# Two chunks side by side in a linear-attention stage, and ranks by two products

## The chip, the cores and the metric

The kernel runs on one core of a Trainium2 chip. The metric is the time of one execution on the device in microseconds; the median of three runs is compared. Names of engines: TensorE (PE; its weight loads are PEld), VectorE (DVE), ScalarE (ACT), GpSimd (POOL) and SyncE (SP), which issues most of the DMAs.

## The reference

The first stage is a retention layer (linear attention with a decay per head) for 4 batches, 8 heads, 768 steps and a head size of 64. Its output, seen as 3072 tokens of 512 features, goes through a mixture of 8 experts: each token goes to its best expert alone.

```python
for t in range(S):
    state = gamma[None, :, None, None] * state + np.einsum('bhd,bhe->bhde', k[:, :, t], v[:, :, t])
    y[:, :, t] = scale * np.einsum('bhd,bhde->bhe', q[:, :, t], state)
...
logits = x @ w_gate + modality_bias[modality_id]
e_idx = np.argmax(logits, axis=1)
...
for e in range(E):
    mask = e_idx == e
    h = np.maximum(x[mask] @ w1[e], 0.0)
    out[mask] = gate_w[mask, None] * (h @ w2[e])
```

## The kernel before, in words

**Retention.** The sequence is cut into chunks of 128 steps: 6 a batch, 24 in all (`NN`). For chunk n the kernel needs five kinds of TensorE products. `scores(n)` (L164) multiplies k and q of all heads, two heads at a time in the two halves of the rows (64*128), into two PSUM banks; VectorE applies the causal mask, which gives the tile `a` (L176). `heads_out(n)` (L182) makes the output y: first the state times q (L189, array of 64*64, four at once; left out in the first chunk of a batch), then v times `a` (L195, 128*64), both into the same two banks; VectorE multiplies them by the decay and writes `yT` (L202). `state(n)` (L222) adds k times v of chunk n to a bank that lives for a batch (L227, 128*64; left out in the last chunk of a batch), and ScalarE copies it to `s` (L232). `tokens_out(n)` (L205) multiplies yT by a matrix that holds the identity and the gate weights (L213, 128*128), in two halves u that have a bank each; ScalarE copies them to `xs`, and VectorE adds up the logits `lg` (L218). GpSimd makes `vd`, v with its decay (L159), ScalarE makes `dq`, the decay for the output (L152).

**The order.** All engines but GpSimd issue exactly in the order of the Python code (`manual_schedule`), GpSimd in the order of its pinned instructions. `retention(n)` (L869) does, on TensorE: state of n, scores of n+1, x of n-1, y of n. Loads are issued on SP nine chunks ahead (`LEAD`); k and q, and k and v, go to rooms that the weights and hidden tiles of the experts use later. Between the steps stand hooks: `at(n, where, ...)` places a function at a point of chunk n ("top", "st", "sc", "pr", "tk", "end").

**Ranking.** Every three chunks make a group. `route_a(g, 0)` and `route_a(g, 1)` (L299) are a serial chain of small VectorE steps: logits plus bias (L303), maximum, one-hot rows `oh`, and the running counts `cnt`. `route_b(g)` (L333) makes each token's place by five products: `upper` times `oh`, a base for each expert (`ebase`), the counts, and two sums over earlier chunks of the group. `route_c` and `route_a(g, 2)` (L349, L327) read the result on VectorE (`rkt`, `pos`, `den`, and three reciprocals). `scatter` (L358) writes each chunk's rows to a list of rows by expert in DRAM (`xsl`). After the group of chunk 11, `early_a` and `early_b` (L440, L448) pick two experts that have a full slot of 512 rows already: one product `pte` and 15 small VectorE steps from `full` to `bid`; `taken_a`, `taken_b` (L474, L479) note it with the tile `tk` and the products `ptk`.

**Experts.** Six jobs of 512 rows follow: two early ones (e0, e1) and four more (f0 to f3), each 192 products of 128x512. `flip` (L668) transposes a job's rows, `cut` (L657) splits weights into a high and a low part, `first` (L680) and `second` (L699) are the two layers. The flips and cuts of e0 are hooks in the last chunks of the retention, with the low parts on GpSimd (L663). `last_tokens` (L898) and the final lists (`final_a` to `final_d`) run between the first products of e0. Small remainders of experts (`rest_*`, L739 to L806) and rows that fill gaps (`gaps_*`) run in between.

Of the kernel before, what the change touches and what calls it, by code (L numbers as in the profile page):

```python
# [40 lines left out]
LEAD = 9  # L41
XSB = 6
# [3 lines left out]
C_ID, C_MASK, C_DEC, C_IOTA, C_FAC, C_GRP, C_LANE, C_END = 0, 128, 256, 304, 312, 336, 337, 356  # L46
# [3 lines left out]
def kernel(  # L50
# [44 lines left out]
    run_base = cst[:, C_LANE + 3 + NE : C_LANE + 3 + 2 * NE]  # L95
# [4 lines left out]
    ebase = cp.tile([P, GRP, NE], BF16, name="ebase")  # L100
# [3 lines left out]
    cnt = [cp.tile([P, NE], BF16, name=f"cnt{i}") for i in range(NGRP + 1)]  # L104
# [6 lines left out]
    kqs, kts, vts, vds, lg, mid, xss = ({} for _ in range(7))  # L111

    kqr = ld.tile([P, 4, 2, DM], F32, tag="kq", name="kqr", bufs=1)


    def load_kq(n, split=False):
        i = n % 12
        if i < 4:
            t = kqr[:, i]
        else:  # L120
            t = me.tile([P, QW], F32R, tag=f"{('hi2', 'lo2')[i // 8]}{i % 4}", name=f"kq_{n}")
            t = t.bitcast(F32).rearrange("p (i d) -> p i d", i=2)
        kqs[n] = t
        if split:
            nc.sync.dma_start(t[:, 0], qkv[n][:, 0])
            nc.scalar.dma_start(t[:, 1], qkv[n][:, 1])
        else:
            nc.sync.dma_start(t, qkv[n][:, 0:2])
# [16 lines left out]
    def decay_q(n):  # L145

        c = n % NCH
        if c == 0:
            return dcq
        t = wk.tile([P, NG, P], F32, tag="dq", name=f"dq_{n}", bufs=1)  # L150
        for g in range(NG):
            nc.scalar.activation(t[:, g], dcq[:, g], AF.Copy, scale=fac[:, c, g : g + 1])  # L152
        return t

    def decay_v(n):
        vv = vts[n].rearrange("p (h e) -> p h e", h=H)
        vds[n] = wk.tile([P, H, D], F32, tag="vd", name=f"vd_{n}", bufs=2)
# [6 lines left out]
    def scores(n):  # L164
        kt, qt = (kqs[n][:, i].rearrange("p (g t) -> p g t", g=NG) for i in range(2))
        a = wk.tile([P, 2, NG, P], F32, tag="a", name=f"a_{n}")
# [13 lines left out]
        return a, qt  # L180

    def heads_out(n, a, vd, qv, s, dq):  # L182
        py = [bank(f"y{j}_{n}")[:, : 2 * P].rearrange("p (c t) -> p c t", c=2) for j in range(2)]
        if s is not None:
            for g in range(NG):
                for j in range(2):
                    r = slice(j * D, (j + 1) * D)
                    h = slice(g % 2 * D, (g % 2 + 1) * D)
                    nc.tensor.matmul(  # L189
# [936 lines left out]
```

## Time and profile before

| what | value |
|---|---|
| median of three runs | 408.42 us (407.78 to 408.92) |
| profiled execution | 407.8 us |
| its span, first to last instruction | 405.9 us |
| VectorE busy | 192.8 us |
| ScalarE busy | 155.0 us |
| GpSimd busy | 100.3 us |

An execution's time is about 1.9 us longer than its span: that is what lies around the instructions. Rows of the timeline give start, duration, engine, line, operation, out<-in, and the count of merged instructions; rows of the chain give start, duration, and what it stood on; rows of groups give a count, busy time, the mean of one in ns, and the idle time before it with what ended it. The ends of products on TensorE are modelled, so two that follow each other overlap in the rows; their starts are what to go by.

### The profile page before, as it was taken

To read this page: it belongs to the slowest core of one execution; us is meant where nothing else is said; L and a number is where in the kernel's file an instruction comes from. 1 tells how busy PE (TensorE), PEld (TensorE's weight loads), DVE (VectorE), ACT (ScalarE), POOL (GpSimd) and SP (SyncE) were. 2 spreads that over 40 slices of the span, in tenths; PEclk is the share of its full clock that TensorE was granted. 3 is DMA by queue.
4 is the path that set the end of the run, shared out by engine and by line. 5 is a ranking of instruction groups with operands and counts; after the bars stand their busy time and mean duration, and the time that the engine had idled before them with its cause. 6 is when DMAs were issued, how large, how long until landed. Compare 5 with 4: busy or idle time off the path is not lost.

```text
span 405.9 us, 8274 instructions
## 1 busy us (share of the span) xinstructions
PE 391.2 (96%) x3099; PEld 324.4 (80%) x3099; DVE 192.8 (48%) x489; ACT 155.0 (38%) x309; POOL 100.3 (25%) x120
## 2 busy tenths in 40 slices
PE   4999999999998999999999999999999999999993
PEld 3888888888886888888887888778888888888882
DVE  1687688879747932346214362143622463234200
ACT  1444544458543423335233252332523352243210
POOL 1326543578552471000110001100011000100011
PEclk9999999999999999999999999999999999999999
DMA  7999999984345484266971669616343453310011
GB/s 274 386 379 414 410 384 368 406 261 177 122 146 200 178 288 153 104 213 195 359 252 53 222 188 375 242 53 214 105 144 115 136 182 131 130 54 2 0 52 49
DMA packets 26795, 82.33 MB, mean 203 GB/s; under 512 B 4733, under 2 KB 4861, under 8 KB 26497
## 3 DMA queue, kind: packets, MB, share of 16 engines
q1 hardware_dynamic: 21328, 66.11, 45.9%
q0 software_dynamic: 5136, 15.21, 9.7%
q8 instruction: 26, 0.43, 0.4%
q10 hardware_dynamic: 288, 0.44, 0.3%
q14 instruction: 17, 0.14, 0.1%
HBM read 65.43 MB, written 23.41 MB: 219 GB/s over the span
## 4 chain that ended last, share of the span: by engine, by line
PE 58%; issue 32%; POOL 4%; DVE 2%; DMA 1%; POOLq 1%; ACT 0%; ACTq 0%; DVEq 0%
PE h_e L686 11%; PE o_e L704 11%; PE x L213 6%; PE sc L171 6%; PE h_f L686 6%; PE y L195 6%; PE o_f L704 4%; POOL out_dram L712 3%; PE y L189 3%; PE st L227 3%; DMA cst<-in_consts_dram 1%; PE xp_e L671 1%; PE xp_f L671 1%; POOL lo_e L663 1%; POOL vd L159 1%
## 5 line engine op out<-in xcount | busy, mean ns | idle before, releaser
L704 PE MATMUL o_f<-hi_f,hT_f 128*128 128x512 f32 x256 | 79.4, 391 | 0.0
L665 DVE TENSOR_TENSOR lo_f<-raw_f,hi_f 128x1024 fp32r<-128x1024 f32 x32 | 39.2, 1225 | 49.6 <-ACT hi_f L660 49.6
L704 PEld LDWEIGHTS o_f<-hi_f,hT_f 128*128 128x128 f32 x256 | 47.6, 188 | 9.6
L694 DVE SCALAR_TENSOR_TENSOR hT_f<-h_f,hT_f 128x512 fp32r<-128x512 f32 x32 | 22.1, 692 | 68.0 <-ACT hT_f L693 68.0
L686 PE MATMUL h_f<-xTh_f,hi_f 128*128 128x512 f32 x128 | 51.0, 399 | 0.0
L686 PE MATMUL h_f<-xTl_f,hi_f 128*128 128x512 f32 x128 | 50.2, 392 | 0.0
L686 PE MATMUL h_f<-xTh_f,lo_f 128*128 128x512 f32 x128 | 50.2, 392 | 0.0
L704 PE MATMUL o_f<-lo_f,hT_f 128*128 128x512 f32 x128 | 49.9, 390 | 0.0
L712 POOL DMA_INDIRECT out_dram<-o_f,tok_f x16 | 15.7, 979 | 133.1 <-ACT o_f L711 118.6
L693 ACT ACTIVATE hT_f<-h_f 128x512 fp32r<-128x512 f32 x32 | 19.1, 598 | 56.6 <-PE h_f L686 55.2
L176 DVE TENSOR_TENSOR a<-sc,cst 128x512 f32<-128x512 f32 x48 | 30.8, 684 | 19.2 <-PE sc L171 19.1
L704 PE MATMUL o_e<-hi_e,hT_e 128*128 128x512 f32 x128 | 39.8, 392 | 0.0
L159 POOL TENSOR_TENSOR vd<-kv,cst 128x512 f32<-128x512 f32 x24 | 25.1, 1045 | 38.4 <-PE y L195 23.7
L711 ACT ACTIVATE o_f<-o_f,gate_f 128x512 f32<-128x512 f32 x16 | 11.0, 689 | 59.9 <-issue 34.3
L660 ACT CAST hi_f<-raw_f 128x1024 fp32r<-128x1024 f32 x32 | 33.4, 1044 | 0.0
L366 POOL DMA_INDIRECT xsl<-xs,pos x24 | 24.4, 1017 | 27.5 <-DVE xs L330 14.4
L686 PEld LDWEIGHTS h_f<-xTh_f,hi_f 128*128 128x128 f32 x128 | 24.0, 188 | 6.4 <-issue 1.2
L213 PE MATMUL x<-wgt,yT 128*128 128x136 f32 x192 | 28.3, 290 | 0.5 <-DVE yT L202 0.5
L686 PEld LDWEIGHTS h_f<-xTl_f,hi_f 128*128 128x128 f32 x128 | 24.0, 188 | 5.5
L686 PEld LDWEIGHTS h_f<-xTh_f,lo_f 128*128 128x128 f32 x128 | 24.1, 188 | 5.1
L704 PEld LDWEIGHTS o_f<-lo_f,hT_f 128*128 128x128 f32 x128 | 24.0, 188 | 5.1
L704 PEld LDWEIGHTS o_e<-hi_e,hT_e 128*128 128x128 f32 x128 | 23.7, 188 | 4.7
(182 smaller groups left out, 623.4 us busy)
## 6 DMA issues: line engine op xcount, KB each, us to landing
raw_f<-in_w_dram SPq DMA_DIRECT2D x32, 512.0 KB, 3.4
kv<-in_qkv_dram SPq DMA_DIRECT2D x19, 512.0 KB, 11.0
kq<-in_qkv_dram SPq DMA_DIRECT2D x16, 512.0 KB, 10.6
raw_e<-in_w_dram SPq DMA_DIRECT2D x16, 512.0 KB, 4.3
xg_f<-xsl SPq DMA_DIRECT2D x16, 272.0 KB, 4.1
kqr<-in_w_dram SPq DMA_DIRECT2D x8, 512.0 KB, 4.6
rw<-in_w_dram SPq DMA_DIRECT2D x8, 512.0 KB, 6.4
kqr<-in_qkv_dram SPq DMA_DIRECT2D x7, 512.0 KB, 11.4
```

Source lines behind the costliest of these rows:

```text
L159: nc.gpsimd.tensor_tensor(vds[n], vv, dec[:, n % NCH].unsqueeze(2).to_broadcast([P, H, D]), op=ALU.mult)
L171: nc.tensor.matmul(pe[j][:, g * P : (g + 1) * P], kt[r, g], qt[r, g], start=True, stop=True, skip_group_check=True,)
L176: nc.vector.tensor_tensor(a[:, j], pe[j].rearrange("p (h t) -> p h t", t=P), mask.unsqueeze(1).to_broadcast([P, NG, P]), op=ALU.mult,)
L195: nc.tensor.matmul(py[j][g % 2 * D : (g % 2 + 1) * D, g // 2], vd[:, 2 * g + j], a[:, j, g], start=(s is None and g < 2), stop=(g >= 2), s ...
L213: nc.tensor.matmul(px[:, g], yT[:, 2 * u + g], wgt[:, 2 * u + g], start=(g == 0), stop=(g == 1), skip_group_check=True,)
L366: ins = nc.gpsimd.indirect_dma_start(out=xsl[:, :], out_offset=bass.IndirectOffsetOnAxis(ap=mid[gr][:, i : i + 1], axis=0), in_=xs.rearran ...
L660: nc.scalar.copy(hi, t)
L665: nc.vector.tensor_tensor(lo, t, hi.bitcast(F32), op=ALU.subtract)
L686: nc.tensor.matmul(s.ph, s.w[1][f // 2][wi][:, o : o + P], s.xT[kc][a], start=(kc == 0 and k == 0), stop=(kc == KC - 1 and k == 2),)
L694: nc.vector.scalar_tensor_tensor(lo, s.ph, 0.0, hi.bitcast(F32), op0=ALU.max, op1=ALU.subtract)
L704: nc.tensor.matmul(s.po, s.hT[f][a][:, hh * P : (hh + 1) * P], s.w[2][f // 2][wi][:, (f % 2) * DM : (f % 2 + 1) * DM], start=(f == 0 and k ...
L712: ins = nc.gpsimd.indirect_dma_start(out=out[:, :], out_offset=bass.IndirectOffsetOnAxis(ap=s.tok[:, hh : hh + 1], axis=0), in_=o[:, :], i ...
```

## The change

Chunks are taken two at a time. `two_chunks(n)` makes on TensorE the scores of n+2 and n+3, x of n-2 and n-1, the state products of y of n and n+1, and then `a` of n, state of n+2, `a` of n+1, state of n+3. `first_chunks()` starts this off. `a` has four rooms of one tile (`abuf`), `vd` four, `s` three, `dq` two, `xs` eight. Loads go twelve chunks ahead, into rooms of the weights (`hi`, `lo`), of xT and of hT; the tiles `kq` and `kv` of their own are gone, and the rests' weights go to `abuf`, `vd`, `yT` and `dq`. The count tiles hold the base of each expert from the start and the running sum before each chunk of the group (`cums`), so `route_b` needs two products; the constants of the lists are changed to suit. A group that is complete at an odd chunk is ranked one chunk later. The flips of e0 move from chunks 19 and 20 to 20 and 22. In `last_tokens` three empty steps are added and `final_a` moves behind `route_c`. The last output tile is scaled half on VectorE and half on ScalarE.

```diff
-LEAD = 9
-XSB = 6
+LEAD = 12
+XSB = 8
...
     def load_kq(n, split=False):
-        i = n % 12
-        if i < 4:
-            t = kqr[:, i]
-        else:
-            t = me.tile([P, QW], F32R, tag=f"{('hi2', 'lo2')[i // 8]}{i % 4}", name=f"kq_{n}")
-            t = t.bitcast(F32).rearrange("p (i d) -> p i d", i=2)
+        tag = f"{('hi', 'lo')[n // 4 % 2]}{1 if n < 8 else 2}{n % 4}"
+        t = me.tile([P, QW], F32R, tag=tag, name=f"kq_{n}")
+        t = t.bitcast(F32).rearrange("p (i d) -> p i d", i=2)
...
     def load_kv(n, split=False):
-        i = n % 10
-        if i < 8:
-            t = me.tile([P, 2, SLOT], F32R, tag=f"hT{i}", name=f"kv_{n}").bitcast(F32)
-        else:
-            t = ld.tile([P, 2, DM], F32, tag="kv", name=f"kv_{n}", bufs=2)
+        tag = f"xT{n - 8}" if n // 4 == 2 else f"hT{(n if n < 8 else n - 12) % 8}"
+        t = me.tile([P, 2, SLOT], F32R, tag=tag, name=f"kv_{n}").bitcast(F32)
...
-            new = sm.tile([P, NE], F32, tag="new", name=f"new_{gr}")
-            nc.vector.tensor_reduce(new, oh.rearrange("p c e -> p e c"), axis=AX.X, op=ALU.add)
-            nc.vector.tensor_tensor(cnt[gr + 1], cnt[gr], new, op=ALU.add)
+            cum = cums[gr]
+            for i in range(GRP):
+                nxt = cum[:, i + 1] if i + 1 < GRP else cnt[gr + 1]
+                nc.vector.tensor_tensor(nxt, cum[:, i], oh[:, i], op=ALU.add)
...
         nc.tensor.matmul(pr, upper, oh, start=True, stop=False, skip_group_check=True)
-        nc.tensor.matmul(
-            pr, ones[0:1, :], ebase[0:1], start=False, stop=False, skip_group_check=True
-        )
-        for i in range(-1, GRP - 1):
-            src = cnt[gr] if i < 0 else oh[:, i]
-            to = GRP - 1 - i
-            nc.tensor.matmul(
-                pr[:, i + 1 :], ones, src.unsqueeze(1).to_broadcast([P, to, NE]),
-                start=False, stop=(i == GRP - 2), skip_group_check=True,
-            )
+        nc.tensor.matmul(pr, ones, cums[gr], start=False, stop=True, skip_group_check=True)
...
         if part == 3:
-            nc.scalar.activation(o, s.po, AF.Copy, scale=s.gate[:, hh : hh + 1])
+            gate = s.gate[:, hh : hh + 1]
+            if s is jobs[-1] and hh == HH - 1:
+                h = DM // 2
+                nc.vector.tensor_scalar(o[:, h:], s.po[:, h:], gate, None, op0=ALU.mult)
+                nc.scalar.activation(o[:, :h], s.po[:, :h], AF.Copy, scale=gate)
+            else:
+                nc.scalar.activation(o, s.po, AF.Copy, scale=gate)
...
     for g in range(NGRP - 1):
         t = (g + 1) * GRP
+        t += t % 2
...
-        at(t + 7 + kc // 2, ("pr", "tk")[kc % 2], flip, e, kc)
+        at(t + 8 + kc // 2 * 2, ("pr", "tk")[kc % 2], flip, e, kc)
...
+    def two_chunks(n):
+        loads(n + LEAD - 2)
+        run(n, "top")
+        ahead = n + 2 < NN
+        if ahead:
+            decay_v(n + 2)
+        decay_q(n)
+        if ahead:
+            scores(n + 2)
+        run(n, "st")
+        loads(n + LEAD - 1)
+        if ahead:
+            scores(n + 3)
+            decay_v(n + 3)
+        run(n, "sc")
+        run(n, "pr")
+        tokens_out(n - 2)
+        run(n, "tk")
+        tokens_out(n - 1)
+        decay_q(n + 1)
+        run(n, "end")
+        run(n + 1, "top")
+        if n % NCH:
+            heads_s(n)
+        heads_s(n + 1)
+        run(n + 1, "st")
+        heads_a(n)
+        if ahead:
+            state(n + 2)
+        run(n + 1, "sc")
+        heads_a(n + 1)
+        run(n + 1, "pr")
+        if ahead:
+            state(n + 3)
+        run(n + 1, "tk")
+        run(n + 1, "end")
```

`heads_s` and `heads_a` are the two halves of `heads_out`, the first with the state, the second with `a` and the step to yT.

**TensorE in the middle of the retention.** Before, around chunks 8 and 9 (st state, sc scores, x tokens, y outputs, by chunk number):

```order
L227 MATMUL st_585<-vd_655,kv_139 64x64 x8
L171 MATMUL sc_9_759<-kq_156 128x128
...
L213 MATMUL x_0_772<-wgt,yT_714 128x136 x2
L213 MATMUL x_1_776<-wgt,yT_714 128x136 x2
L189 MATMUL y_8_781<-kq_137,s_665 64x128
...
L195 MATMUL y_8_781<-a_672,vd_655 64x128 x4
L195 MATMUL y_8_782<-a_672,vd_655 64x128 x4
L227 MATMUL st_585<-vd_737,kv_158 64x64 x8
L171 MATMUL sc_10_832<-kq_201 128x128
```

Now, in the pair of chunks 8 and 9:

```order
L166 MATMUL sc_10_762<-kq_148 128x128
...
L166 MATMUL sc_11_782<-kq_152 128x128
...
L219 MATMUL x_0_798<-wgt,yT_704 128x136 x2
L219 MATMUL x_1_802<-wgt,yT_704 128x136 x2
L219 MATMUL x_0_808<-wgt,yT_725 128x136 x2
L219 MATMUL x_1_812<-wgt,yT_725 128x136 x2
L190 MATMUL y_8_830<-kq_140,s_581 64x128
...
L190 MATMUL y_9_840<-kq_144,s_715 64x128
...
L202 MATMUL y_8_830<-abuf,vd_600 64x128 x4
L238 MATMUL st_551<-vd_755,kv_150 64x64 x8
L202 MATMUL y_9_840<-abuf,vd_634 64x128 x4
```

Blocks of one kind now stand next to each other for two chunks, and the state of chunk 10 stands between the two outputs.

**VectorE at the early list.** Before, behind the group of chunk 11 (yT of chunk 13, the list from `full` to `bid`, the ranking's second half from `rkt`, the note `tk`, then the masks of chunk 15):

```order
L202 TENSOR_TENSOR yT_1174<-y_13_1157,dq_1127 128x256
L451 TENSOR_TENSOR full_1185<-pte_1183,full_at 1x48
...
L352 TENSOR_TENSOR rkt_1211<-rk_1177,oh_1106 128x24
...
L476 TENSOR_SCALAR tk<-bid 1x48
L176 TENSOR_TENSOR a_1288<-sc_15_1289,cst 128x512
L176 TENSOR_TENSOR a_1288<-sc_15_1290,cst 128x512
```

Now:

```order
L209 TENSOR_TENSOR yT_1173<-y_13_1129,dq_1104 128x256
L452 TENSOR_TENSOR full_1191<-pte_1189,full_at 1x48
...
L353 TENSOR_TENSOR rkt_1217<-rk_1186,oh_1123 128x24
...
L171 TENSOR_TENSOR abuf<-sc_16_1234,cst 128x512
L171 TENSOR_TENSOR abuf<-sc_16_1235,cst 128x512
L477 TENSOR_SCALAR tk<-bid 1x48
L171 TENSOR_TENSOR abuf<-sc_17_1292,cst 128x512
L171 TENSOR_TENSOR abuf<-sc_17_1293,cst 128x512
```

The list and the second half stood ahead of one chunk's masks; now they stand ahead of the four masks of chunks 16 and 17, with `tk` in their midst. On TensorE the next pair's x of chunk 13, whose second half takes the bank that the first scores of chunk 16 leave, and then the products of `tk`, come after these scores:

```order
L166 MATMUL sc_17_1292<-kq_618 128x128
...
L219 MATMUL x_0_1312<-wgt,yT_1152 128x136 x2
L219 MATMUL x_1_1316<-wgt,yT_1152 128x136 x2
L219 MATMUL x_0_1322<-wgt,yT_1173 128x136 x2
L219 MATMUL x_1_1326<-wgt,yT_1173 128x136 x2
L483 LDWEIGHTS ones
L483 MATMUL ptk<-tk,ones 48x48
...
L190 MATMUL y_14_1351<-kq_429,s_1029 64x128
```

Before, these small products stood behind a chunk's outputs; now they stand between x and the outputs of the pair.

More of the change, by code (lines that the diff above doesn't have):

```diff
@@ L103 @@
     cnd = cp.tile([NCAND, 2 * NCAND + 3], F32, name="cnd")
-    cnt = [cp.tile([P, NE], BF16, name=f"cnt{i}") for i in range(NGRP + 1)]
+    cums = [cp.tile([P, GRP, NE], BF16, name=f"cum{i}") for i in range(NGRP + 1)]
+    cnt = [t[:, 0] for t in cums]
     def pin(ins):
@@ L179, in scores, with y_banks, heads_s, heads_a @@
             )
[L180 to L189, printed above, removed]
-                        py[j][h, g // 2], s[r, g], qv[r, g], start=(g < 2), stop=False,
-                        skip_group_check=True,
-                    )
+    def y_banks(n):
+        pys[n] = [
+            bank(f"y{j}_{n}")[:, : 2 * P].rearrange("p (c t) -> p c t", c=2) for j in range(2)
+        ]
+    def heads_s(n):
+        y_banks(n)
+        py, s = pys[n], ss.pop(n - 1)
+        qv = kqs[n][:, 1].rearrange("p (g t) -> p g t", g=NG)
+        for g in range(NG):
+            for j in range(2):
+                r = slice(j * D, (j + 1) * D)
+                h = slice(g % 2 * D, (g % 2 + 1) * D)
+                nc.tensor.matmul(
+                    py[j][h, g // 2], s[r, g], qv[r, g], start=(g < 2), stop=False,
+                    skip_group_check=True,
+                )
+    def heads_a(n):
+        first = n % NCH == 0
+        if first:
+            y_banks(n)
+        py, vd, a, dq = pys.pop(n), vds.pop(n), az.pop(n), dqs.pop(n)
         for j in range(2):
@@ L220, in tokens_out, with state @@
         )
-    def state(n, st, vd):
+    def state(n):
+        c = n % NCH
+        if c == NCH - 1:
+            return
+        if c == 0:
+            ss["st"] = bank(f"st_{n}")[:, : NG * D].rearrange("p (g e) -> p g e", g=NG)
+        st, vd = ss["st"], vds[n]
         kk = kts[n].rearrange("p (h d) -> p h d", h=H)
-        c = n % NCH
         for g in range(NG):
@@ L850 @@
         at(t + 2, "end", scatter, g, 1)
-        at(min(t + 3, NN - 1), "end" if t + 3 == NN else "st", scatter, g, 2)
+        at(t + 3, "st", scatter, g, 2)
     t = GRP * min(EARLY)
@@ new lines, in two_chunks, with first_chunks @@
+        if ahead:
+            state(n + 3)
+        run(n + 1, "tk")
+        run(n + 1, "end")
+    def first_chunks():
+        scores(0)
+        decay_v(1)
+        state(0)
+        run(0, "st")
+        scores(1)
+        run(0, "sc")
+        decay_q(0)
+        decay_q(1)
+        heads_a(0)
+        decay_v(2)
+        run(0, "end")
+        run(1, "top")
+        state(1)
+        run(1, "st")
+        scores(2)
+        run(1, "sc")
+        decay_v(3)
+        heads_s(1)
+        heads_a(1)
+        run(1, "end")
+        state(2)
+        scores(3)
+        state(3)
@@ L898, in last_tokens @@
     def last_tokens():
         g = NGRP - 1
-        tokens_out(NN - 1, carry["y"])
+        tokens_out(NN - 1)
+        run(NN, "st")
         yield
+        run(NN, "end")
+        run(NN + 1, "st")
+        assert not hooks, hooks
         yield
         route_a(g, 0)
+        yield
         yield
@@ L907, in last_tokens @@
         yield
+        yield
         route_b(g)
-        final_a()
         yield
@@ L912, in last_tokens @@
         route_a(g, 2)
+        final_a()
         scatter(g, 0)
+        yield
         yield
@@ L994 @@
         at(2, "sc", setup_rows)
-        at(9, "end", setup_stores)
+        at(8, "end", setup_stores)
         at(3, "sc", setup_c)
         at(4, "sc", list_consts)
-        for n in range(NN):
-            retention(n)
-        assert not hooks, hooks
+        first_chunks()
+        for n in range(2, NN, 2):
+            two_chunks(n)
+        tokens_out(NN - 2)
         r = last_tokens()
```

104 lines of the change are left out of this document (40 added, 64 removed).

## The prediction

> **What bounds the kernel now.** I read the page first: TensorE is busy all the time.
>
> ```profile
> span 405.9 us, 8274 instructions
> PE 391.2 (96%) x3099; PEld 324.4 (80%) x3099; DVE 192.8 (48%) x489; ACT 155.0 (38%) x309; POOL 100.3 (25%) x120
> ```
>
> Then the timeline of TensorE, for the place where the experts begin: their first product starts at 113.50. Everything behind it is a stream of 128x512 products that the change does not touch, so the question is at what time that product starts, plus small edits behind it.
>
> ```profile
> 12.99 1.16 PE L171 MATMUL sc<-kqr 64*128 64x128 f32 x16
> ...
> 113.50 0.50 PE L686 MATMUL h_e<-xTh_e,hi_e 128*128 128x512 f32 x1
> ```
>
> Up to the first of these rows (the scores of chunk 2) both kernels issue the same products in the same order, so I let the sum run from 12.99 to 113.50, which is 100.5 us now. Third, the chain that ended last, in order of time, around chunks 7 to 10:
>
> ```profile
> 41.02 1.02 PE y L195 x16
> 42.04 0.12 PE rk L336
> 42.16 0.11 PE rk L337
> 42.27 0.16 PE rk L343 x3
> 42.44 0.61 PE st L227 x16
> ...
> 45.87 1.02 PE y L195 x16
> ...
> 47.35 1.09 PE sc L171 x16
> 48.45 1.12 PE x L213 x8
> 49.57 0.60 PE y L189 x16
> 50.17 1.02 PE y L195 x16
> ```
>
> The chain stays on TensorE: a chunk takes 50.17 - 45.87 = 4.30 us, and no other engine is on it. Fourth, the inside of each block of products: pieces of TensorE's timeline from the middle of a block (start, duration to the last end, count), and the mean of one product.
>
> ```profile
> 21.92 0.84 PE L171 MATMUL sc<-kq 64*128 64x128 f32 x12
> 61.55 0.86 PE L213 MATMUL x<-wgt,yT 128*128 128x136 f32 x6
> 23.97 0.51 PE L189 MATMUL y<-kqr,s 64*64 64x128 f32 x12
> 24.57 0.82 PE L195 MATMUL y<-a,vd 128*64 128x128 f32 x12
> 25.39 0.58 PE L227 MATMUL st<-vd,kv 128*64 128x64 f32 x14
> ...
> L195 PE MATMUL y<-a,vd 128*64 128x128 f32 x384 | 26.8, 282 | 0.0
> L213 PE MATMUL x<-wgt,yT 128*128 128x136 f32 x192 | 28.3, 290 | 0.5 <-DVE yT L202 0.5
> L227 PE MATMUL st<-vd,kv 128*64 128x64 f32 x320 | 13.5, 228 | 1.4 <-POOL vd L159 1.4
> ```
>
> Scores run in pairs, each product about 0.28 long as the others of 128 columns: (0.84 - 0.28) / 5 = 0.112 us from pair to pair, so 8 pairs are 0.90. In the same way x is 8 x (0.86 - 0.29) / 5 = 0.91, y with the state (fours) 4 x (0.51 - 0.28) / 2 = 0.46, y with the masked scores (pairs) 8 x (0.82 - 0.28) / 5 = 0.87, st 8 x (0.58 - 0.228) / 6 = 0.47. The sum is 3.6, and the chunk takes 4.30: 0.70 us per chunk are lost where one kind of product follows another. There are four such changes, 0.17 each; from y (L195) to st, which have the same shape of array (128*64), there is none (0.47 for st is its pure length, while behind a rank product it takes 0.61).
>
> **The change part by part.** *Pairs.* In a pair TensorE has sc sc, x x, ys ys, then ya st ya st: four changes for two chunks instead of eight. That x's second half in another bank follows the first at the same 0.114 says that a new bank or a wait already satisfied does not break a block. From st back to ya no row exists; I take 0 as for ya to st, with 0.17 (ten pairs, 1.7 us) as the other end. A pair is then 8.60 - 0.70 = 7.90.
>
> A rule of the Trainium skill speaks against this: TensorE: Matmul & The Clock Gate, What overlaps and what doesn't, says that a weight load overlaps running matmuls only where the row group differs. By it x, ya and st, which use all 128 rows, could not close up across two chunks; but inside x blocks this trace has products of 0.29 following each other in 0.114, each with its own load, so I keep the rows.
>
> The nine pairs from chunks 4, 5 to chunks 20, 21: 9 x 7.90 = 71.1; three first chunks of a sequence have no ys (3 x 0.46 = 1.4 less), three pairs lack one st (1.4 less); the flips of the first expert's rows stay:
>
> ```profile
> 91.88 0.59 PE xp_e L671 x4
> 92.47 0.93 PE x L213 x8
> 93.40 0.44 PE xp_e L671 x4
> ```
>
> Two of them lengthen a chunk by 0.59 + 0.44 - (1.12 - 0.93) = 0.8. *Ranks.* Five products now cost 0.39 us (rows of 42.04 to 42.44), and 0.54 where they part ya and st. Two products in the place of a change that is there anyway: 0.12 to 0.35, I take 0.25; six pairs, 1.5, and 0.2 for the early list's three small products. Sum 70.8.
>
> *The start.* Scores are wanted two chunks earlier, while loads still arrive at the speed of the DMA queues:
>
> ```profile
> 10.00:20.00 10.00, 10.00 (x154) 8.90 (x152) 6.63 (x19) 4.64 (x14) 3.73 (x5) 1.00 1.02 386
> ...
> 14.11 0.34 SPq L128 DMA_DIRECT2D kq<-in_qkv_dram  x1
> ...
> DMA to landing us min/median/max: 7.2/7.2/7.2
> ```
>
> The DMA share is 1.02, and the load of k and q of chunk 5, issued at 14.11, lands at 21.3. SP issues the first nine chunks in the same order in both, so that stays; the three chunks more of LEAD queue behind it. From 12.99 the new order needs sc2 1.09, ys1 0.60, ya1 1.02, st2 0.47, sc3 1.09, st3 0.61, sc4 1.0: 18.9, so sc5 waits 2.4 us for its load; now it comes too late for that to matter. After 21.3: sc5 1.0, x x 2.0, ys ys 1.0, ya st ya 2.4: the pair of chunks 4, 5 starts at 27.7, and without any further wait the last pair at 27.7 + 70.8 = 98.5.
>
> *VectorE.* Its steps keep their lengths but stand in another order, and scores' banks come free only by its masks. The rows for one ranking step and the early list:
>
> ```profile
> 63.82 0.79 DVE L303 TENSOR_TENSOR lg<-lg,tbias 128x24 f32<-128x24 f32 x1
> ...
> 65.94 0.17 DVE L322 TENSOR_TENSOR cnt<-cnt,new 128x8 bf16<-128x8 bf16 x1
> 66.03 1.28 DVE L176 TENSOR_TENSOR a<-sc,cst 128x512 f32<-128x512 f32 x2
> ...
> 67.45 0.75 DVE L202 TENSOR_TENSOR yT<-y,dq 128x256 f32<-128x256 f32 x2
> 68.28 0.20 DVE L451 TENSOR_TENSOR full<-pte,full_at 1x48 f32<-1x48 f32 x1
> ...
> 71.17 0.16 DVE L352 TENSOR_TENSOR rkt<-rk,oh 128x24 f32<-128x24 f32 x1
> ...
> 72.20 0.16 DVE L476 TENSOR_SCALAR tk<-bid 1x48 bf16<-1x48 f32 x1
> ```
>
> So the first half of a ranking step (L303 to L322) is 2.2 us, 2.4 with one small addition more; the early list 2.9; the second half (L352 to L330) 1.0; two masks 1.28; one yT 0.75. In the pair of chunks 12, 13 the first half begins once x of chunk 11 is copied and reduced, about 4.7 us after the pair's start (four x halves from 2.0 to 4.0, then ScalarE's copy and a short reduce): to 7.1, two yT to 8.6, early list to 11.5, second half to 12.5, then the masks of 16 at 13.2 and 13.8. TensorE, whose pair is 7.75 long, wants at 7.75 + 3.4 = 11.2 the bank of the first of these masks for x of chunk 13, and then the list's tk: ys starts at about 14.2 instead of 11.8. **Wait 2.4 us**, once. Before, the same list stood between masks and yT of single chunks, and no one waited. In the other ranking pairs the second half (1.0 us, from about 1.2 to 2.2 of the pair) stands ahead of the masks, done at 2.9, 3.5, 4.1, 4.8, and ys wants their banks from 4.0 on: 0 to 0.6 us each, I take 0.3 in four pairs: 1.2.
>
> *GpSimd.* The four lo parts of the first expert stand between the vd; before, that costs a stall too:
>
> ```profile
> 86.71 2.35 POOL lo_e L663
> 89.06 1.00 POOL vd L159
> ```
>
> In the pair of chunks 20, 21 two lo, two scatters and vd of 22 are queued; I take 0.2 us (0 to 1.5). The loads of chunks 16 to 23 wait for k and q eight chunks older, so they have over 15 us to land: nothing. So the last pair starts at 98.5 + 2.4 + 1.2 + 0.2 = 102.3.
>
> *The last pair* has flips and x 2.9, ys 1.1, ya 1.8, ranks 0.25, that is 6.05; VectorE's first half there runs from about 3.7 (x of chunk 21, copied) to 6.1, and yT of 22 is ready half by half from 6.5 on, so a wait of about 0.5, then x 1.1: the first expert product at 102.3 + 7.7 = 110.0. **Gain 3.5** (113.5 - 110.0).
>
> *Behind it.* The last rank loses three products (0.2). final_a moves behind the second half; its wait stays about as long as it is:
>
> ```profile
> PE pcf L411 <- DVE crepf L408: 1.3, 1, 1.3
> ...
> 399.50 0.69 ACT L711 ACTIVATE o_f<-o_f,gate_f 128x512 f32<-128x512 f32 x1 [4.75 <-PEq L1009]
> ```
>
> The last output in two halves, VectorE beside ScalarE: a 128x256 read of a bank is about 0.4 (yT above) instead of 0.69, gain 0.25, as only a scatter follows. The rooms of the rests, gaps and weights change names, under a TensorE that streams: nothing, with half a microsecond if a rest's load came late. Together 0.4: **3.9 us in all**. The profiled execution took 407.8, so 403.9; the median of the runs shown, 408.42, is 0.6 above it, and I forecast 404.3.
>
> **The rivals.** *No waits on VectorE* (27%): its rows have slack or the banks fall better; then 2.4 + 1.2 go: 400.7. For it: VectorE is busy 48%. Against: in the ranking pairs four masks 2.6, four yT halves and two reduces 2.0, halves 2.4 + 1.0, together 8.0 us of the pair's 8.1. *Blocks of all 128 rows do not close up* (6%): then only scores and ys save, 0.36 of 0.70 a pair, and 11 x 0.34 = 3.7 are lost: 408.0, no change. That is what the rule above would make of it. *The first expert is not ready* (5%): its last flips move from chunk 20 to the last pair, some 6 us ahead of their use; if rows or weights came as late as before, the 3.5 are lost: 407.8. *VectorE becomes the bound* (8%), the rival on the other side: the same row of 8.0 us against 8.1. It decides if each ranking pair's masks come another 0.6 us or more late: L303, a step on 24 columns, took 0.79 here, so such steps can be slow; two more of them in each of six ranking pairs that put TensorE off by 1.0 us each cost 6 us: 410.3. The gain is gone at 0.65 each. The Trainium skill, TensorEngine Tiling (Array Packing), PSUM Bottleneck, says that packing speeds up TensorE but not the emptying of its banks, which may become the bottleneck; in the waits of before TensorE never waits for a mask.
>
> **How the numbers follow.** My forecast has 50%, and 4% lie between. The likeliest case by itself spans 401.7 (the small waits at 0, half of the early list's) to 407.2 (0.17 at each return to ya, 0.6 at each ranking pair). The range reaches down to the case without waits and up to 407.9, where the no-change rivals lie: 400.6 to 407.9. About 0.3%, 1.2 us, is what can be told from no change, so faster is below 407.2: 50 + 27 + 2 = 79%; the same 6 + 5 + 2 = 13%; slower 8%.
>
> **What would show it.** In the profile after: sc x32 in about 2.0, x x16 in about 2.0 on the chain; ya to the next ya about 1.35; one wait of scores for a kq load before 21.4; TensorE waiting for VectorE between the scores of 17 and ys of 14, near 70 to 75 us; two rank products in about 0.25; h_e at about 110. Wrong it is if pairs of blocks keep a step of 0.2 inside, if no wait for VectorE stands there (then faster), or if h_e waits for xT or weights.

## The result and the profile after

The changed kernel takes 410.50 us (median of 10 runs, 409.32 to 412.64), the kernel before 408.47 (10 runs): a ratio of 1.0052, 95% interval 1.0033 to 1.0072. It is slower by half a per cent where 404.3 was forecast, and lies outside the range. The profiled execution has a span of 407.5 us. In three of the six jobs of the experiments (a job is a set of kernels run together on one chip) TensorE's completions reached the other engines late; the kernel before took 408.9 to 409.4 us there and 408.1 to 408.2 in the other three, so a ratio is always one against the kernel before of the same job.

The first expert product starts at 117.39 instead of 113.50: 3.9 us later, not 3.5 earlier. Behind it 2.3 us are won (290.1 to the end of the span instead of 292.4). So the stage of the pairs lost, and the stage of the experts gained more than foreseen.

First TensorE's timeline for one undisturbed pair, chunks 10 and 11 (start, duration, engine, line, operation, count):

```profile
51.36 2.06 PE L166 MATMUL sc<-kq 64*128 64x128 f32 x32
53.35 2.12 PE L219 MATMUL x<-wgt,yT 128*128 128x136 f32 x16
55.40 1.10 PE L190 MATMUL y<-kq,s 64*64 64x128 f32 x32
56.43 1.09 PE L202 MATMUL y<-abuf,vd 128*64 128x128 f32 x16
57.36 0.63 PE L238 MATMUL st<-vd,kv 128*64 128x64 f32 x16
57.82 1.04 PE L202 MATMUL y<-abuf,vd 128*64 128x128 f32 x16
58.70 0.63 PE L238 MATMUL st<-vd,kv 128*64 128x64 f32 x16
59.26 0.19 PE L346 MATMUL rk<-oh,upper 128*128 128x24 bf16 x1
59.30 0.17 PE L347 MATMUL rk<-cum,ones 128*128 128x24 bf16 x1
59.41 0.83 PE L166 MATMUL sc<-kq 64*128 64x128 f32 x10
```

59.26 - 51.36 = 7.90: the pair is exactly as long as predicted, and the two rank products take 59.41 - 59.26 = 0.15, less than the 0.25 assumed. The change does what it says. Then TensorE's waits in the whole program (for whom; total us, times, longest):

```profile
PE sc L166 <- DMA kq<-in_qkv_dram: 6.9, 2, 5.1
PE rk L347 <- DVE cum L332: 3.0, 1, 3.0
PE ptk L483 <- DVE tk L477: 1.5, 1, 1.5
PE x L219 <- DVE abuf L171: 0.8, 1, 0.8
PE xp_e L671 <- DVE abuf L171: 0.7, 1, 0.7
PE pte L443 <- DVE cum L332: 0.6, 1, 0.6
PE x L219 <- DVE rkt L353: 0.6, 1, 0.6
```

Before, TensorE waited for VectorE twice: 0.5 in the retention and 1.3 for `final_a` behind it. Now the six waits for VectorE listed here, 7.2 us in all, stand in place of the 0.5 (the other is still there, at 0.9, and scores wait 0.2 once). TensorE's timeline at two of the places (the bracket is the idle time ahead and what ended it):

```profile
73.25 0.73 PE L219 MATMUL x<-wgt,yT 128*128 128x136 f32 x4 [0.75 <-DVE abuf L171]
75.50 0.23 PE L483 MATMUL ptk<-tk,ones 1*48 1x48 bf16 x1 [1.52 <-DVE tk L477]
75.67 1.98 PE L190 MATMUL y<-kq,s 64*64 64x128 f32 x32
77.58 1.56 PE L202 MATMUL y<-abuf,vd 128*64 128x128 f32 x16
...
99.50 0.18 PE L347 MATMUL rk<-cum,ones 128*128 128x24 bf16 x1 [2.99 <-DVE cum L332]
99.61 3.40 PE L166 MATMUL sc<-kq 64*128 64x128 f32 x32
```

And VectorE, then GpSimd, at the same places:

```profile
73.72 1.73 DVE L477 TENSOR_SCALAR tk<-bid 1x48 bf16<-1x48 f32 x1
...
96.17 3.48 DVE L332 TENSOR_TENSOR cum<-cum,oh 128x8 bf16<-128x8 bf16 x3
...
101.88 2.32 DVE L338 TENSOR_SCALAR den<-den 128x3 f32<-128x3 f32 x1
```

```profile
74.35 1.05 POOL L154 TENSOR_TENSOR vd<-kv,cst 128x512 f32<-128x512 f32 x1
...
97.07 2.35 POOL L663 TENSOR_TENSOR lo_e<-raw_e,hi_e 128x1024 fp32r<-128x1024 f32 x1
...
100.81 2.36 POOL L663 TENSOR_TENSOR lo_e<-raw_e,hi_e 128x1024 fp32r<-128x1024 f32 x1
103.12 1.04 POOL L154 TENSOR_TENSOR vd<-kv,cst 128x512 f32<-128x512 f32 x1
```

Steps that take 0.17 us elsewhere take 1.73, 3.1 (one of the three cum) and 2.32, and each ends within 0.1 us of the end of a tensor operation of GpSimd: 75.45 and 75.40, 99.45 (the chain gives that cum as 96.36, 3.10) and 99.42, 104.20 and 104.16. Two of the three begin ahead of the recorded start of that tensor operation (73.72 against 74.35, 96.36 against 97.07), while GpSimd is still at an indirect DMA, and stand still from there on. A second loss shows behind the waits: ys takes 1.98 instead of 1.10, scores 3.40 instead of 2.06. The windows there (stretch; length, busy times and counts of PE, PEld, DVE, ACT, POOL; granted clock; DMA share; GB/s):

```profile
75.00:77.00 2.00, 1.50 (x26) 1.48 (x30) 2.00 (x7) 0.58 (x2) 1.64 (x4) 0.54 0.35 138
77.00:79.00 2.00, 2.00 (x32) 1.67 (x28) 0.30 (x2) 0.00 (x0) 0.99 (x1) 0.61 0.89 244
...
99.00:101.00 2.00, 1.50 (x13) 1.39 (x14) 1.97 (x13) 0.00 (x0) 1.69 (x4) 0.51 0.21 61
101.00:103.00 2.00, 2.00 (x25) 1.88 (x22) 1.93 (x6) 0.00 (x0) 2.00 (x1) 0.63 0.87 336
```

The granted clock is about one half for some 3.4 us behind each of the two long waits, and 1.00 around them. By that, each such stretch costs up to 1.7 us. The ten runs of this kernel have a mean clock of 0.979 to 0.987, those of the kernel before in the experiments 0.994 to 0.999.

### The profile page after: what moved, and what is told of

It reads as the page before. It is cut to its first block, busy times and chain, and to the rows that moved or that the text cites. A ratio compares the mean times of both kernels' runs of the same rounds, so it can differ in the third digit from the quotient of the medians.

```text
span 407.5 us, 8242 instructions
## 1 busy us (share of the span) xinstructions
PE 385.2 (95%) x3075; PEld 324.4 (80%) x3075; DVE 199.8 (49%) x496; ACT 156.6 (38%) x309; POOL 100.4 (25%) x120
## 4 chain that ended last, share of the span: by engine, by line
PE 53%; issue 32%; DMA 5%; DVE 5%; POOL 3%; POOLq 1%; ACT 0%; ACTq 0%; DVEq 0%
PE o_e L704 11%; PE h_e L686 10%; PE h_f L686 6%; PE o_f L704 5%; PE x L219 5%; PE y L202 5%; PE sc L166 4%; POOL out_dram L718 3%; PE y L190 3%; DMA kq<-in_qkv_dram 2%; DMA kv<-in_qkv_dram 2%; PE st L238 1%; DMA cst<-in_consts_dram 1%; PE xp_f L671 1%; PE xp_e L671 1%
## 5 line engine op out<-in xcount | busy, mean ns | idle before, releaser
L686 PE MATMUL h_f<-xT_f,hi_f 128*128 128x512 f32 x256 | 81.3, 393 | 0.0
L686 PEld LDWEIGHTS h_f<-xT_f,hi_f 128*128 128x128 f32 x256 | 48.0, 188 | 11.1 <-issue 1.2
L694 DVE SCALAR_TENSOR_TENSOR hT_f<-h_f,hT_f 128x512 fp32r<-128x512 f32 x32 | 22.1, 692 | 66.4 <-ACT hT_f L693 66.4
L686 PE MATMUL h_f<-xT_f,lo_f 128*128 128x512 f32 x128 | 49.9, 390 | 0.0
L686 PE MATMUL h_e<-xT_e,hi_e 128*128 128x512 f32 x128 | 41.0, 395 | 0.0
L171 DVE TENSOR_TENSOR abuf<-sc,cst 128x512 f32<-128x512 f32 x48 | 30.0, 680 | 14.1 <-PE sc L166 14.1
L166 PE MATMUL sc<-kq 64*128 64x128 f32 x384 | 29.0, 303 | 7.2 <-DMA kq<-in_qkv_dram 6.9
L166 PEld LDWEIGHTS sc<-kq 64*128 64x128 f32 x384 | 26.0, 210 | 11.7 <-DMA kq<-in_qkv_dram 5.4
L223 ACT COPY xs<-x 128x272 f32<-128x272 f32 x48 | 18.6, 387 | 26.7 <-PE x L219 15.0
L686 PEld LDWEIGHTS h_e<-xT_e,hi_e 128*128 128x128 f32 x128 | 24.0, 188 | 4.9
```

Source lines behind the costliest of these rows:

```text
L166: nc.tensor.matmul(pe[j][:, g * P : (g + 1) * P], kt[r, g], qt[r, g], start=True, stop=True, skip_group_check=True,)
L171: nc.vector.tensor_tensor(a[:, j], pe[j].rearrange("p (h t) -> p h t", t=P), mask.unsqueeze(1).to_broadcast([P, NG, P]), op=ALU.mult,)
L686: nc.tensor.matmul(s.ph, s.w[1][f // 2][wi][:, o : o + P], s.xT[kc][a], start=(kc == 0 and k == 0), stop=(kc == KC - 1 and k == 2),)
L694: nc.vector.scalar_tensor_tensor(lo, s.ph, 0.0, hi.bitcast(F32), op0=ALU.max, op1=ALU.subtract)
```

## Theories

**A.** A step of VectorE whose operands lie in SBUF stands still while GpSimd's tensor operations run. In the new order these steps stand ahead of something that TensorE waits for, and half speed follows the waits. **B.** VectorE is simply too full in the ranking pairs: the prediction's rival of 410.3, whatever holds its steps. A side question is where the 1.8 us among the experts come from.

## Experiments

The first four kernels ran beside each other (kernel before: 408.12).

**GpSimd without the low parts.** In the changed kernel:

```diff
-            pin(nc.gpsimd.tensor_tensor(lo, t, hi.bitcast(F32), op=ALU.subtract))
+            lo = hi
```

> The changed kernel without GpSimd's four subtractions for the low parts of e0's first weights (2.35 us each); the high part is used in their place, so this part of the computation is left out. Theory A, VectorE's steps with both operands in SBUF stand still as long as GpSimd's tensor operations run: the steps of 3.1 and 2.3 us at 96 and 102 us shrink to 0.2, TensorE's wait of 3.0 for the running sums goes, with it about 2 us of slow products behind it; about 405.5 (404.5 to 406.5). Theory B, VectorE simply has too much work in the ranking pairs (its own steps and their order): the wait stays, 409 or more.

405.48, ratio 0.9926 (0.9902 to 0.9950). As A has it: the 3.1 and 2.3 us steps are gone from its trace, and with them the wait of 3.0; VectorE's own work in the retention was not touched.

**GpSimd without any tensor operation in the retention.** As above, and

```diff
-        vds[n] = wk.tile([P, H, D], F32, tag="vd", name=f"vd_{n}", bufs=4)
-        pin(nc.gpsimd.tensor_tensor(vds[n], vv, ..., op=ALU.mult))
+        vds[n] = vv
```

> As the run without the low parts, and GpSimd's multiplication of v by its decay left out as well (v itself is used), so that GpSimd has no tensor operation in the retention; this part of the computation is left out, and other tokens may go to other experts. Theory A: no small VectorE step is longer than 0.25 us any more; the wait for tk (1.5) and the slow products behind it (1.4) go too; first expert product near 108.5, time about 402. Theory B: chains stay late, first expert product at 114 or later.

401.34, ratio 0.9843 (0.9823 to 0.9863), first expert product at 109.18. VectorE's timeline for the same step tk, between the same neighbours:

```profile
72.06 0.17 DVE L472 TENSOR_SCALAR tk<-bid 1x48 bf16<-1x48 f32 x1
```

0.17 instead of 1.73. An indirect DMA of GpSimd runs at that time here too (71.65 to 72.64), so that alone does not hold the step; why some steps stand still ahead of the recorded start of a tensor operation stays open. No small VectorE step up to the first expert product is over 0.15 us above its shortest; in the changed kernel eight are, by 10.2 us together, and tk by 1.6. Behind the first expert product the two kernels agree (289.8 and 290.1), so the gain is the retention's. A holds. What stays of B is the list's chain itself: x of chunk 13 still waits 0.75 for the mask behind it. Two more waits, 1.37 and 0.32 in the pair of chunks 20, 21, stand behind VectorE's copies that wait for the first expert's rows (a load from 84.56 on, 9.95 us to its landing): the prediction's rival of a first expert that is not ready, which shows only where nothing else is late.

**The note of the taken experts later.** In the changed kernel, t = 12:

```diff
-    at(t + 2, "st", taken_a)
-    at(t + 2, "end", taken_b)
+    at(t + 8, "sc", taken_a)
+    at(t + 9, "end", taken_b)
```

> The changed kernel with the note of the taken experts (tk, ptk and two copies) moved from the pair of chunks 14, 15 to the pair of chunks 20, 21. Theory A: the wait of 1.5 us for tk goes and most of the 1.4 us of slow products behind it, about 408 (407.5 to 408.8). Theory B, the serial list of early_b alone sets when scores' banks come free: the wait for the masks stays and grows by what tk took, 409.5 to 410.5.

405.50, ratio 0.9943 (0.9921 to 0.9965): a larger gain than A's 407.5 to 408.8. The wait for tk and both half-speed stretches went. By luck of timing the running sums were then no longer behind a low part of GpSimd either: which step is caught depends on a few tenths of a microsecond. In its new place tk took 2.08, again beside GpSimd, and TensorE waited 1.7 behind it.

**The flipped rows in one tile.** In the kernel before:

```diff
-        hi = me.tile([P, SLOT], F32R, tag=f"xTh{kc}", name=f"xTh{kc}_{s.tag}")
-        lo = me.tile([P, SLOT], F32R, tag=f"xTl{kc}", name=f"xTl{kc}_{s.tag}")
+        t = me.tile([P, 2, SLOT], F32R, tag=f"xT{kc}", name=f"xT{kc}_{s.tag}")
+        hi, lo = t[:, 0], t[:, 1]
```

> The kernel before with one edit: the high and low part of an expert's flipped rows (xTh, xTl) are two halves of one tile, as in the changed kernel. In the changed kernel a product of the first layer follows the other in 0.2302 us on the mean instead of 0.2335. Theory that the shared tile does this: 576 first-layer products of the six jobs by 0.0033 give 1.9 us, so about 406.6. Rival, that the step comes from something else (order of work, the clock, other rooms): no change, 408.4.

407.74, ratio 0.9994 (0.9982 to 1.0005), and the step is 0.2335 in the first layer's first half as before. The shared tile is not it.

The next job (kernel before: 408.89) is one of the three with late completions.

**The two-product ranks alone**, in the kernel before (the diff's lines on cums, route_b and the constants):

```diff
+        nc.tensor.matmul(pr, ones, cums[gr], start=False, stop=True, skip_group_check=True)
```

> The kernel before with the two-product ranks alone (running sums on VectorE, base in the counts). Theory of the prediction: a rank falls from 0.39 to 0.15 us as the changed kernel's trace has it, 0.54 to 0.15 where it parts ya and st: seven ranks in the retention and one in e0, about 2.0 us in all, so 406.2. Rival: VectorE's chain in front of the ranks grows by one step of 0.2 us and is hit by GpSimd elsewhere, so that nothing is left: 408.1.

407.71, ratio 0.9975 (0.9962 to 0.9988): 1.0 us (0.5 to 1.6) won, half of what was expected. The ranks are short, but the first expert product starts at 113.45, no earlier than in the first job's trace of the kernel before (113.50). The last rank starts at 109.70 (109.81 there), and the wait for yT behind it is 0.8 instead of 0.5. No trace of the kernel before was kept in a job with late completions, so where the 1.0 us lies is not shown.

**One load earlier**, in the changed kernel:

```diff
         load_kq(4)
+        load_kq(5)
         load_kv(4)
         setup_loads()
-        load_kq(5)
```

> The changed kernel with one load moved: k and q of chunk 5 are loaded ahead of k and v of chunk 4 and of the small loads. If the scores of chunk 5 wait for that load (the third term of the prediction, 2.4 us), it lands about 1.4 us earlier and the pair of chunks 4, 5 starts near 26.8 instead of 28.1; the time falls to about 409.1. Rival: the load of k and v behind it is then the late one, or the pairs behind wait for VectorE anyway: 410.5.

The pair of chunks 4, 5 starts at 26.72 (26.8 expected, 28.14 in the changed kernel). The time is 408.30 (409.1 expected), ratio 0.9977 (0.9945 to 1.0009), and the runs fall into two kinds, five of each: 405.8 to 406.9 with a mean clock of 0.994 to 0.998, and 409.7 to 411.6 with 0.984 to 0.988. The work is the same, so the spread goes with the half-speed stretches.

**Ranks and list half a pair later**, in the changed kernel:

```diff
-        at(t + 1, "end", route_b, g)
+        r = (t + 2, "sc") if t + 2 < NN else (t + 1, "end")
+        at(*r, route_b, g)
...
-        at(t + 1, "end", route_c, g)
-        at(t + 1, "end", route_a, g, 2)
-        at(t + 2, "st", scatter, g, 0)
+        at(*r, route_c, g)
+        at(*r, route_a, g, 2)
+        at(t + 2, "tk", scatter, g, 0)
...
```

> The changed kernel with only the order of the ranks changed: the two rank products, the list's product, early_b and the second half of a ranking step come half a pair later, behind the next pair's scores and masks, tk at the end of the pair of chunks 14, 15 and ptk in the pair behind it. No VectorE step is removed and GpSimd does the same work. Theory A: the loss comes from TensorE queued behind VectorE's stretched chains; with slack in front of the rank products the waits (0.6, 0.6, 0.8, 1.5, 3.0, 0.7) and the two slow stretches of TensorE (1.7 us each) go, about 402 (401 to 404). Theory B, VectorE is the bound of the ranking pairs: the chains then delay masks and yT instead, 406 or more.

**All together**: this order, the earlier load, the low parts behind a pair's vd, and ScalarE alone for the last output:

```diff
-        at(t + 5 + i, "end", cut, e, 1, i, True)
+        at(*((t + 6, "sc"), (t + 7, "end"), (t + 8, "sc"), (t + 9, "end"))[i], cut, e, 1, i, True)
```

> The late ranks, the earlier load of k and q of chunk 5, the low parts of e0 on GpSimd queued behind the vd of a pair, and the last output tile scaled by ScalarE alone again. Theory A: late ranks 402, the load 1.3 less, the waits for vd 1 less, the tail 0.2 less: about 399.5. Theory B: 404 or more, since VectorE and GpSimd hold each other up anyway.

413.91 (ratio 1.0097, 1.0067 to 1.0127) and 408.49 (0.9978, 0.9959 to 0.9998): both far above what A gave. The first keeps one wait of 3.6 for VectorE, whose step L338 stands 4.25 us beside GpSimd; the rest is of another kind. TensorE's and ScalarE's waits in it:

```profile
PE st L238 <- issue: 3.8, 2, 3.0
```

```profile
ACT s L243 <- remote: 3.8, 1, 3.8
```

The products of st had started at 70.67 and, by their durations, were over at 71.3, but their completion reached ScalarE at 74.66. In the first job's traces no wait up to the first expert product ends in such a way. So the two ran again, beside the changed kernel and the late note, in another job (kernel before: 408.15).

> The changed kernel once more, as the measure for the other three of this job. In the job of the late ranks TensorE's completions reached the other engines up to 2.7 us late, in bursts, which the traces of the first job do not show. Theory that this belongs to the chip or moment of that job: here again either none, and 410.5, or the same bursts in this kernel too, and 412 or more. Theory that the late order causes it: none in this kernel, 410.5, and bursts again in the two late orders.

411.88, ratio 1.0074 (1.0043 to 1.0106).

> The late ranks once more. Without the late completions (2.5 at 72 us with a slow stretch of TensorE behind it, and several of 1 to 2) the time is 413.9 less about 7: 407, against 410.5 of the changed kernel; what stays is a wait of 3.6 for VectorE, whose den step stood 4.2 us behind three tensor operations of GpSimd. If the order itself makes the completions late: 413 to 414.

407.11, ratio 0.9973 (0.9952 to 0.9993).

> Late ranks, earlier load, low parts behind vd, ScalarE alone at the end, once more. Without the late completions (1.7 and 2.5 us, and 3.4 for the slow stretch of TensorE behind the second) about 408.5 less 9: 399.5. If the order itself makes them late: 408 to 409.

404.81, ratio 0.9907 (0.9876 to 0.9937).

> The changed kernel with the note of the taken experts moved to chunks 20, 21, beside the changed kernel on one chip: 5.0 less than it, as before (405.5 against 410.5). If the first difference came from two chips: less than 2.

404.83, ratio 0.9925 (0.9903 to 0.9948); one of its five runs took 409.32, at half speed for 6.8 us near the start.

No late completions here: for these orders they belong to the job. The late ranks gain 4.8 us on the changed kernel, all together 7.1, and the late note 7.1. The late ranks' 407.11 is what was expected of the second run, but 5 us above A's first figure of 402 and in the range that was B's: their trace has a wait of 4.0 for VectorE, whose step L338 stands 4.69 us beside GpSimd. So A has the mechanism right, and not the number. The third was expected at 399.5 and stands at 404.8. VectorE, GpSimd and TensorE in its trace say why:

```profile
95.28 4.56 DVE L338 TENSOR_SCALAR den<-den 128x3 f32<-128x3 f32 x1
```

```profile
93.14 2.39 POOL L663 TENSOR_TENSOR lo_e<-raw_e,hi_e 128x1024 fp32r<-128x1024 f32 x1
95.48 2.04 POOL L154 TENSOR_TENSOR vd<-kv,cst 128x512 f32<-128x512 f32 x2
97.48 2.33 POOL L663 TENSOR_TENSOR lo_e<-raw_e,hi_e 128x1024 fp32r<-128x1024 f32 x1
```

```profile
100.88 1.13 PE L190 MATMUL y<-kq,s 64*64 64x128 f32 x14 [4.43 <-DVE xT_e L677]
```

One step on three columns stands 4.56 us behind four operations of GpSimd in a row (to 99.81), and TensorE waits 4.43. In this order the standstill falls on another step that TensorE waits for.

The changed kernel's slowest runs show the clock a third time: in this job's trace the wait of 1.73 for k and q of chunk 5 is followed by half speed, while the same 1.73 left the clock at 1.00 in the first trace. Its window and TensorE's timeline:

```profile
22.00:26.00 4.00, 3.94 (x24) 3.75 (x25) 1.29 (x2) 0.39 (x1) 1.63 (x3) 0.50 1.00 354
```

```profile
24.07 3.99 PE L219 MATMUL x<-wgt,yT 128*128 128x136 f32 x16
```

x takes 3.99 instead of 2.12, and the pair of chunks 4, 5 starts at 31.65 instead of 28.14.

**Without the one step**, in the version with all together and in the changed kernel (kernel before: 408.24):

```diff
-            nc.vector.tensor_scalar(den, den, 1e-9, None, op0=ALU.add)
```

> The version with late ranks, earlier load, low parts behind vd and ScalarE alone at the end, without the step that adds 1e-9 to the sum of exponentials (L338, 0.17 us when alone; the sum is never under 1, so the step changes nothing in this format). In its last run this step stood 4.6 us behind four tensor operations of GpSimd, TensorE waited 4.4 for VectorE, and 6.8 us at half speed followed. Theory A, a step with its operands in SBUF waits for GpSimd while the steps beside it that read PSUM or sum up do not: wait and slow stretch go, 404.8 less 4.4 less 2.5: about 398 (396.5 to 399.5). Theory B, VectorE is full in these pairs: the next step takes the wait over, 402 or more.

401.77, ratio 0.9821 (0.9794 to 0.9847): the fastest version here that leaves nothing out, 1.8% under the kernel before. The 4.4 us went, as A has it, but the time is 3.8 above A's 398 and close to B's 402: as B said, the next step took a wait over. TensorE's waits in it:

```profile
PE sc L166 <- DMA kq<-in_qkv_dram: 5.9, 4, 5.1
PE rk L345 <- DVE oh L326: 2.2, 1, 2.2
```

The first step of the last ranking (L312) now takes 2.98 beside the last low part, and 6.8 us at half speed follow. So it is again GpSimd that holds the step, and not a full VectorE.

> The changed kernel without that one step. Theory A: in the pair of chunks 20, 21 the masks start 2.3 us earlier, TensorE's waits of 0.7 and about 0.6 go, and up to 0.5 of the slow stretch: about 409.5; the larger waits (tk, running sums) stay as they are. Theory B: no change, 410.5 to 412.

407.84, ratio 0.9996 (0.9970 to 1.0021), lower than either theory had it. In the trace the stretch from the scores of chunk 22 to the first expert product is 1.1 us shorter (16.7 instead of 17.8), as A has it. The median lies further below the changed kernel's two (410.50 and 411.88) than that explains.

**The last low part earlier.**

```diff
-        at(*((t + 6, "sc"), (t + 7, "end"), (t + 8, "sc"), (t + 9, "end"))[i], cut, e, 1, i, True)
+        at(*((t + 6, "sc"), (t + 8, "top"), (t + 8, "sc"), (t + 8, "tk"))[i], cut, e, 1, i, True)
```

> The version without the step L338, with GpSimd's low parts of e0 moved once more: the last one comes in the pair of chunks 20, 21 instead of at its end, where it held the first step of the last ranking (2.98 us instead of 0.17), TensorE waited 2.2 for it, and 6.8 us at half speed followed. Theory A: that wait and the slow stretch go, 401.8 less 2.2 less 3.4: about 396.5 (395 to 398.5). Theory B: the low parts then hold the vd or the scatters, 400 or more.

408.97, ratio 0.9992 (0.9972 to 1.0012; kernel before 409.42; one of twelve runs took 415.49), in a job with late completions, so it ran once more:

> The version with the last low part of GpSimd moved ahead, once more: its first run fell into a job in which TensorE's completions reached the other engines late (2.3 to 2.5 us in two places, 0.3 to 0.6 in others), as in the job of the late ranks. Theory A, without these: 396.5 to 399.5 against 401.8 of the version before it. Theory B, the order itself makes them late, or the low parts hold the vd: 405 or more.

409.72, ratio 1.0017 (1.0000 to 1.0034; kernel before 409.38). Both times are in B's range and far above A's. Both traces show late completions of up to 3.3 us at the same two places, and half speed behind each. VectorE's steps are 2.3 us over their shortest in all, none of them waited for. This order never ran in an undisturbed job, so whether it is the faster one there, and whether the order has a part in the late completions, stays open.

**Two layouts of the kernel before**, for the first layer's products: rooms taken ahead of everything for half of the weights, and 128 bytes ahead of everything.

```diff
+        for i in (2, 3):
+            for nm in ("hi", "lo"):
+                t = me.tile([P, QW], F32R, tag=f"{nm}1{i}", name=f"{nm}1{i}_room")
+                nc.gpsimd.memset(t.bitcast(F32)[:, 0:1], 0.0)
```

> The kernel before with the rooms of the third and fourth pair of first-layer weights allocated ahead of everything else, so that all weights and the flipped rows lie at other addresses; nothing else differs. In the kernel before a first-layer product takes 0.2335 us in the first half of each job (first two pairs of weights) and 0.2267 in the second half; in the changed kernel 0.2267 throughout. If the addresses decide: the pattern of halves changes. If something else in the first half of a job decides: 0.2335 and 0.2267 as before.

```diff
+    pad = cp.tile([P, 32], F32, name="pad")
+    nc.gpsimd.memset(pad, 0.0)
```

> The kernel before with 128 bytes of room put ahead of everything, so that every tile lies 128 bytes later. In the three programs so far a first-layer product took 0.2267 us where its weights start at 32 in steps of 256 bytes of a partition, and 0.2335 where they start at 160. If that place alone decides: the halves of a job change roles, 0.2267 first and 0.2335 in the second half. If the distance to the flipped rows decides, which stays: 0.2335 first, 0.2267 second, as before.

The first took 409.81 (one run), with 0.2335 in both halves; the second 408.54 (one run), with 0.2335 and then 0.2267. So the rooms decide, and it is the distance between them. By the addresses in the built programs, taken in steps of 256 bytes, weights and flipped rows start 128 bytes apart where a product takes 0.2335, and at the same place where it takes 0.2267. That holds in all four layouts (before, these two, and the changed kernel, where all start at the same place); with the padding the halves kept their times although their places were exchanged.

## Why the prediction was wrong

**Pairs: right.** 7.90 predicted and measured; the return from st to ya costs nothing (57.36 to 57.82 for st, its pure length). The rival by which blocks of all 128 rows do not close up, 408.0, does not hold here.

**Ranks: right, a little better.** 0.15 instead of 0.25.

**Start: right, with a rider.** The scores of chunk 5 wait for their load until 21.6, and the pair of chunks 4, 5 starts at 28.1 (27.7 predicted). That half speed can follow this wait was not seen.

**VectorE: wrong, and this is the step that failed.** The prediction says "Its steps keep their lengths but stand in another order". They do not keep them. The first of the ranking rows that it quotes, L303 with 0.79, was the sign: GpSimd's timeline of the kernel before has, ending at 64.57 as that step ends at 64.61,

```profile
63.53 1.04 POOL L159 TENSOR_TENSOR vd<-kv,cst 128x512 f32<-128x512 f32 x1 [0.89 <-PE y L195]
```

So the 2.2 that it counts for the first half of a ranking step has 0.62 of such a standstill in it: without one, this half takes 1.8 in the changed kernel (85.09 to 86.85). In the kernel before eight steps are held so, by 6.5 us together, and only one of them, L306, stands at the head of a wait of TensorE, the one of 0.5:

```profile
106.24 1.58 DVE L306 TENSOR_TENSOR lg<-lg,mx 128x24 f32<-128x24 f32 x1
```

In the changed kernel nine are held, by 11.8 us with tk, and TensorE waits behind four. The Trainium skill has the rule, SBUF — State Buffer, SBUF: two separate sides: VectorE and GpSimd share a pair of ports that one instruction locks for its whole length, on VectorE's side one with two SBUF inputs or in a mode that uses both ports. The traces agree (by the changed kernel's lines): held are L312, L315, L322, L326, L332 (two inputs in SBUF), L338 and L477 (scalar steps), by 0.2 to 4.5 us over all runs; not held beside the same operations are the maxima and sums L314, L324 and L337, the reciprocals L340, the copies of one column (L649, L650) and all that read PSUM (L171, L209, L353). So theory A, which speaks of any operand in SBUF, is too wide. Whether the two scalar steps run in a mode that uses both ports, no run here shows.

By place: the pair of chunks 14, 15 takes 12.60 (67.81 to 80.41) instead of about 7.5, 5.1 more, and 0.6 are lost ahead of it, where 2.4 were predicted. The pairs of chunks 18 to 21 take 22.1 (88.45 to 110.58) where 15.8 were due (7.6 with a rank and without one ys, 8.2 with the flips and without one st), 6.3 more, where GpSimd's 0.2 was predicted. The small waits in four other ranking pairs (1.2) did not come, the last pair took 6.8 instead of 7.7, and the ranks saved 0.6 more than assumed. From 110.0: + 0.4 + 3.3 + 6.1 - 1.2 - 0.9 - 0.6 = 117.1, and 117.4 was measured. The waits that the prediction did price, 2.4 behind the early list and 1.2 behind the masks, were too high: without GpSimd's tensor operations 0.75 is left of the first and, of the second, 0.32 behind the late rows.

**TensorE's speed: not in the prediction at all.** Of these losses about 1.4 us in each of two stretches is half speed. The Trainium skill, TensorE: Matmul & The Clock Gate, What's actually happening, gives half speed after about 3.4 us of idleness. Here a single wait of 2.99 was enough, and so were 0.57, 0.75 and 1.52 within 4.3 us; the measurement decides.

**GpSimd: the right engine, the wrong effect.** It was counted for vd being late (0.2). It cost through VectorE; TensorE's wait for vd is 0.2, the size predicted.

**Behind the first expert product: wrong in size, 2.3 instead of 0.4.** The rooms were put at nothing and gave about 1.8 (0.28 to 0.35 in each job). The last output was put at 0.25 won; VectorE, ScalarE and GpSimd at the end show

```profile
400.89 0.48 DVE L714 TENSOR_SCALAR o_f<-o_f,gate_f 128x256 f32<-128x256 f32 x1 [20.37 <-PE o_f L704]
...
401.46 0.47 ACT L715 ACTIVATE o_f<-o_f,gate_f 128x256 f32<-128x256 f32 x1 [5.27 <-DVE o_f L714]
402.21 0.98 POOL L718 DMA_INDIRECT out_dram<-o_f,tok_f  x1 [4.76 <-ACTq L1064]
```

ScalarE waits for VectorE's half, so the halves run one behind the other: 7.03 from the start of the last product to the end of the span instead of 6.86.

**The rivals.** The one on the other side, VectorE as the bound at 410.3 with 8%, came within 0.2 us, and its point ("such steps can be slow") was right; the number is luck. Its price was taken as 1.0 a pair in six pairs; it fell on three places instead, 12.0 in all, and gains elsewhere made up for the difference. The rival without waits, 400.7, is near the 401.34 of the run without GpSimd's tensor operations, by luck too: it puts the first expert product at 106.4 (110.0 less 3.6), and there it started at 109.18; the stretch behind it, 2.2 us shorter than forecast, made up for most of that.

**The forecast.** The sum's own last step, 408.42 less 3.9, gives 404.5; the 404.3 stands between that and 403.9.

What stays open: what makes completions late in some jobs (two jobs on the same chip differ, so it is not the chip alone), the exact share of idle time at which the clock falls, and why a step can stand still ahead of the recorded start of GpSimd's operation.

## What to carry to other kernels

A small step that takes several times its usual length is a finding: look at what ends when it ends, on every engine, before counting on its usual length in a new order. When an order removes TensorE's slack, price not only its waits but also the slow stretch behind each. A version that is faster by timing alone can lose it again by a shift of a few tenths.

## What was not expected of the hardware

Half speed can follow waits shorter than 3 us, and lasts some 3.4 or 6.8 us. A product of 128x512 takes 0.2335 or 0.2267 us, as weights and moving rows start 128 bytes apart or together, in steps of 256 bytes: 1.8 us in this program. In some jobs a completion of TensorE reaches its waiters up to 3.4 us after the product's modelled end: the late ranks took 413.91 in one job and 407.11 in another.
